# First products of two expert steps, moved into the attention stage's list

## The chip, the cores and the metric

The kernel is one program on one core of a Trainium2 chip. A core has five engines that run their own instruction lists in order and wait for each other by semaphores: TensorE (PE, matrix products; its weight loads are shown apart as PEld), VectorE (DVE), ScalarE (ACT), GpSimd (POOL) and SyncE (SP, which here only issues transfers, or DMAs). The metric is the device time of one execution in microseconds; lower is better. The kernel before ran at 891.88 us, the median of three runs (890.82, 891.88 and 893.85).

## What is computed

Three parts follow each other, all in fp32 accuracy:

```
attn_out = softmax(causal(q k^T / 8 + decay)) v        # 4 batches, 8 heads, 576 rows, 64 columns
x   = tokens: 2304 rows of 512
e   = argmax(x @ w_gate)                               # one of 8 experts for each token
x2  = weight(x, e) * (relu(x @ w1[e]) @ w2[e])         # 512 -> 1024 -> 512
out = (sigmoid(x2 @ w_gate2) * (x2 @ w_val)) @ w_out   # 512 -> 1536 -> 512
```

The tokens of an expert have to be gathered before its products: each token's row is written to a place that depends on how many tokens of that expert came before it, and rows are read back expert by expert.

## The kernel before, in words

**Attention stage** (`attention`, L740). The work of 16 pairs of heads is added to a list (`Flow.add`) with an assumed cost for each engine; a planner (`Flow.order`) then fixes one order for all engines, and `emit` writes it out. Pairs 12 to 15 are the last batch. When the last pair's `turn_x` (L436, writes `px`) and `scale` (L446, writes `xb`) are done, DVE adds up the expert logits and finds each token's expert (`first`, L591 to L596, the last of it a memset of `ohb`). PE then counts tokens per expert (`prefix`, L602 to L607, bf16 products into `px`), DVE turns the counts into places (`place`, L612 to L616) and weights (`weight`, L631 and L632), and POOL writes the rows of the last batch to `x_d` with five indirect DMAs (`scatter`, L647).

**Ahead of the experts.** After three batches the expert with most tokens so far is known. Its first 216 tokens (`AHEAD`) are fetched, turned and split into a high and a low half (`xah`, `xal`) while the attention stage still runs (`ahead_rows`), and so are the weights of its first three steps (`ahead_steps`: `wa0`, `wa1`, `wa2`).

**Expert stage** (`moe`, L963). It is written out in program order, not planned. A block is a group of tokens of one expert, a step is one eighth of the expert's 1024 hidden columns, and there are 72 steps. Block 0 (steps 0 to 7) is those 216 tokens, block 1 (steps 8 to 15) another 128 tokens of the same expert, among them tokens of the last batch. Step s is: `hidden(s)` (L1036, 12 products into `ph`: high by high, high by low, low by high, over four slices of 128), `relu(s)` (ACT L1042 writes `ha..h`, DVE L1043 `ha..l`), `split(s+2)` (ACT L986 and DVE L987 split a raw weight tile), `down(s-1)` (L1068 to L1070, 12 products into `py`). So PE runs hidden(0), hidden(1), down(0), hidden(2), down(1) and so on. Between these, DVE runs the some 35 small operations of `offsets` (L803 to L877), one at each `next(offsets)`.

**The queue of transfers.** `load(s)` (L981) reads the 512 KB of step s into one of three `raw` buffers, so it waits until `split(s-3)` has emptied its buffer. `fetch(1)` (L998) reads block 1's rows (`xr`) from `x_d` and waits for all scatters. Both are issued by SP, in order: a waiting transfer holds all that stand behind it. `weigh(1, 0)` (ACT L1008, writes `xg`) runs at step 6, `turn(1, 0)` (PE L1020) at step 7, ahead of down(6), and its result, split by ACT L1024 and DVE L1025 into `xh` and `xl`, is what hidden(8) multiplies.

Of the kernel before, what the change touches and what calls it, by code (L numbers as in the profile page):

```python
# [7 lines left out]
F32 = mybir.dt.float32  # L8
# [3 lines left out]
AF = mybir.ActivationFunctionType  # L12
ALU = mybir.AluOpType
# [3 lines left out]
P = 128  # L17
B, H, S, D = 4, 8, 576, 64
NP = B * H // 2
# [6 lines left out]
NK = DM // P  # L26
# [19 lines left out]
AHEAD = ((B - 1) * S + E - 1) // E  # L46
# [190 lines left out]
class Kern:  # L237
# [150 lines left out]
    def attn_pair(self, pr):  # L388


        nc, F, R = self.nc, self.F, self.R
        b, p = divmod(pr, NPB)
        i = pr % 2
        q, k = self.qk[pr]
# [34 lines left out]
        def finish(ts, oT, n):  # L429

            px = R["px"].new()

            def turn_x(e):
                for i in range(len(ts)):
                    for h in range(0, n, 64):
                        nc.tensor.matmul(px.t[h:h + 64, i], lhsT=oT.t[:, i * P + h:i * P + h + 64], rhs=self.w2[:, p],  # L436
                                         start=True, stop=True)
            F.add(turn_x, {"PE": 272 * len(ts)}, r=[oT, "w2"], w=[px], group=pr, kind="x", mode="columns")
            o = xb[:n, ts[0]:ts[-1] + 1, 2 * p:2 * p + 2, :]
            x = px.t[:n, 0:len(ts)].rearrange("p t (j c) -> p t j c", j=2)  # L440
            w = [("xb", b % 2, p, t) for t in ts]
            if ts[0] < 4:
                u = [2 * TORD.index(t) + j for t in ts for j in range(2)]

                def scale(e):
                    nc.vector.tensor_tensor(  # L446
                        out=o, in0=x, op=ALU.mult, in1=rs.t[:, u[0]:u[-1] + 1].rearrange(
                            "p (t j) -> p t j", j=2).unsqueeze(3).to_broadcast([P, len(ts), 2, XW]))
                F.add(scale, {"DVE": 70 + 166 * len(ts)}, r=[px] + [(rs, i) for i in u], w=w, group=pr, kind="scale")
            else:  # L450
                F.add(lambda e: self.copy(e, o, x), {"ACT": 190, "DVE": 240}, r=[px], w=w, group=pr, kind="x")
# [263 lines left out]
    def ahead_steps(self):  # L715
# [7 lines left out]
        for fb in range(NAHEAD):  # L723
# [8 lines left out]
            for i, cs in enumerate((slice(0, DM), slice(DM, 2 * DM))):  # L732
# [4 lines left out]
                    out=l, in0=raw[:, cs], in1=h.bitcast(F32), op=ALU.subtract),  # L737
                    {"DVE": 600, "POOL": 1230}, r=["raw", ("wah", fb, i)], w=[("wal", fb, i)], group=g)

    def attention(self, pool):  # L740
        ac, tmp = pool("ac", 1), pool("tmp", 1)
        F = self.F = Flow(PERIOD, SLACK)
        self.vt, self.qk, self.decay = {}, {}, {}
        spec = {
            "q": ([P, S], 3), "k": ([P, S], 3), "cb": ([P, 2, S], 2), "cm": ([P, 2, 512], 2), "ct": ([P, S], 2), "sc": ([P, 512], NSC), "sct": ([P, S], 1),
            "pt": ([P, 4, 2 * P], NPT), "ptt": ([P, 4, P], 1), "vt": ([P, 4, DM], 2),
            "oT": ([P, 2 * P], 2), "sums": ([P, 9], 3), "nmx": ([P, 9], 3), "rs": ([P, 9], 3),
            "lg": ([P, 5, 2 * E], 2), "m": ([P, 5], 2), "m2": ([P, 5], 2), "ls": ([P, 5, E], 2),
            "pos": ([P, 5, E], 2), "se": ([P, 5], 2), "so": ([P, 5, E], 2), "sel": ([P, 5], 2),
        }  # L750
        self.R = {n: Ring(pool(n, k), n, s, F32, k) for n, (s, k) in spec.items()}
        self.R["ohb"] = Ring(pool("ohb", 2), "ohb", [P, 5, E], BF16, 2)
        for n, s, k in (("px", [P, 2, 2 * XW], NPX), ("ps", [P, 512], NPS), ("tp", [P, 4, P], NTP), ("po", [P, 2 * P], NPO)):
            self.R[n] = Ring(pool(n, k, space=PSUM), n, s, F32, k)
        self.attn_setup(ac, tmp)
        for e in range(E):
            F.add(lambda e_, e=e: self.blank(e), {"SP": 700}, r=["zr"], w=["blank"], group=1 + e // 4, move=2500, after=35e3 + 5e3 * e)
        for i in range(4):
            F.add(lambda e, i=i: self.clear(i), {"SP": 700}, r=["zr"], w=["clear"], group=9 + i, move=2500, after=110e3 + 12e3 * i)
        for pr in range(NP + 2):  # L760
            if pr > 1:
                self.attn_pair(pr - 2)
            if pr < NP:
                self.attn_operands(pr)
        self.ahead_steps()
        F.emit()

    def unordered(self, key, ins):
# [194 lines left out]
    def moe(self, pools, preps):  # L963
        nc = self.nc
# [6 lines left out]
        raw, hs, ex, xg, py = {}, {}, {0: self.aex, 1: self.aex}, {}, {}  # L971
        w, xs = dict(enumerate(self.wa)), {0: self.xa}
        wbuf = self.wa + [[wp.tile([P, 2 * DM], F32R, name=f"w{n}{i}") for n in "hl"] for i in range(4 - NAHEAD)]

        def load(s):
            if s < len(steps):
                q, fb = steps[s]
                if q not in ex:
                    ex[q] = self.reg(self.orderi, blocks[q][2], ET.SP, E - 1)
                raw[s] = rawp.tile([P, 2 * DM], F32, name="raw")  # L980
                nc.sync.dma_start(out=raw[s], in_=self.words(ex[q], fb))  # L981
# [7 lines left out]
        def chunks(q):  # L989
            n = blocks[q][1]  # L990
            return [(c * P, min(n, (c + 1) * P)) for c in range((n + P - 1) // P)]

        def fetch(q):
            a0, _, r = blocks[q]
            row = self.reg(self.firsti, r, ET.SP, (E - 1) * NTOK) if r else self.arow
            for c, (a, b) in enumerate(chunks(q)):
                t = xg[q, c] = xp.tile([P, H, XW], F32, name="xr", bufs=NCH)
                ins = nc.sync.dma_start(  # L998
                    out=t[:b - a].rearrange("p h c -> p (h c)"), in_=self.x_d[bass.ds(row + (a0 + a), b - a)])
                self.after("scatter", ins)  # L1000

        def weigh(q, c):
            a, b = chunks(q)[c]
            t = xg[q, c]
            o = xg[q, c] = xp.tile([P, DM], F32, name="xg", bufs=3)
            o3, x3, g = o[:b - a].rearrange("p (h d) -> p h d", h=H), t[:b - a, :, 0:D], t[:b - a, 0, D:D + 1]
            if q == 1:
                nc.scalar.activation(o3, x3, AF.Copy, scale=g)  # L1008
            else:
                nc.gpsimd.tensor_scalar_mul(o3, x3, g)  # L1010
# [16 lines left out]
        def hidden(s):  # L1027
            q = steps[s][0]
            (wh, wl), (xh, xl), n = w[s], xs[q], blocks[q][1]
            ph = psH.tile([P, 512], F32, name="ph")  # L1030
            mm = []
            for k in range(NK):
                a, b = wh[:, k * P:(k + 1) * P], wl[:, k * P:(k + 1) * P]
                mm += [(a, xh[:, k, :n]), (a, xl[:, k, :n]), (b, xh[:, k, :n])]
            for i, (a, b) in enumerate(mm):
                nc.tensor.matmul(ph[:, :n], lhsT=a, rhs=b, start=i == 0, stop=i == len(mm) - 1)  # L1036
            return ph[:, :n]

        def relu(s, ph):
            n = blocks[steps[s][0]][1]  # L1040
            hh, hl = (t[:, :n] for t in self.ha[s % 2])
            nc.scalar.activation(hh, ph, AF.Relu)  # L1042
            nc.vector.scalar_tensor_tensor(  # L1043
                out=hl, in0=ph, scalar=0.0, in1=hh.bitcast(F32), op0=ALU.max, op1=ALU.subtract)
            hs[s] = hh, hl
# [46 lines left out]
        for s, (q, fb) in enumerate(steps):  # L1092
            if s >= NAHEAD - 1:
                load(s + 1 + NRAW)
            if s == 4:
                fetch(1)
            if (q, fb) == (nb - 1, 0):
                self.most = self.reg(self.nch, E, None, MAXCH)
            nq, c = q + 1, fb - (LATE, 3, 4)[min(q, 2)]
            if s == LATE or fb == 0 and 2 < nq < nb:  # L1100
                fetch(max(nq, 2))
            n = len(chunks(nq)) if nq < nb else 0
            ph = hidden(s)
            next(offsets, None)
            t = None
            if 0 <= c < n:
                t = turn(nq, c)
            early = 1 + (q > 1)
            if q and 0 <= c + early < n:
                weigh(nq, c + early)  # L1110
            relu(s, ph)
            if not q and 0 <= c + 1 < n:
                weigh(nq, c + 1)
            next(offsets, None)
            if t:
                land(*t)
            if s >= NAHEAD - 1:
                split(s + 2)
            if (q, fb) == (2, 2):
                prep = preps(lambda s: self.now >= due(s))  # L1120
            self.now = q, fb
            self.drip()
            if q > 1 and fb > 1:
                next(prep, None)
                if fb % 2:
                    next(prep, None)
            if flat:
                upright(*flat)
            flat = down(s - 1) if s else None
            next(offsets, None)  # L1130
# [525 lines left out]
```

## Time and profile before

| what | us |
|---|---|
| median of three runs | 891.88 |
| lowest, highest | 890.82, 893.85 |
| the profiled execution | 894.48 |
| its span, first to last instruction | 892.7 |
| PE busy in it | 851.7 (95%) |
| PE idle at the end of attention (217.4 to 219.85) | 2.50 |
| stretch behind it at half the granted clock | 6.55 |

All times of rows are microseconds from the start of the profiled span. A row of a timeline is one instruction, or several equal ones merged: start, duration, engine, source line, operation, what it writes and reads, and in square brackets how long the engine stood idle before it and what ended that. The granted clock is a share of TensorE's full 2.4 GHz, so 0.50 is 1.2 GHz.

### The profile page before, as it was taken

How to read it: one execution, taken by the hardware profiler on the slowest of the kernel's cores; microseconds unless marked ns; L12 is line 12 of the kernel's file. 1: busy time of each engine (PE TensorE's matmuls, PEld its weight loads, DVE VectorE, ACT ScalarE, POOL GpSimd, SP SyncE). 2: the span in 40 equal slices, each digit the busy share in tenths (PEclk: the TensorE clock that was granted, in tenths of full speed). 3: DMA queues.
4: the chain of work that ended last, by engine and by line, in shares of the span. 5: the costliest groups of instructions: out<-in, count | busy, mean ns of one | idle time of the engine just before them, and what ended most of it. 6: DMA issues, size and time to landing. Idle time of an engine off the chain costs nothing.

```text
span 892.7 us, 16050 instructions
## 1 busy us (share of the span) xinstructions
PE 851.7 (95%) x5664; PEld 751.5 (84%) x5664; DVE 617.7 (69%) x1439; ACT 449.0 (50%) x986; POOL 304.4 (34%) x380
## 2 busy tenths in 40 slices
PE   4999999998999999999989999999999999999996
PEld 3666667665999999999989888888999999999995
DVE  4767786877675767858747678889898996334454
ACT  3877777785464454646545544434343442332220
POOL 3211331221222222142125527375534466322113
PEclk9999999999999999999989999999999999999999
DMA  7799869543688677597644787757574557655531
GB/s 232 233 285 278 264 163 278 161 151 119 223 262 291 228 240 251 166 318 243 221 130 118 175 177 157 197 107 186 160 248 138 147 180 288 243 204 213 211 130 72
DMA packets 84987, 180.53 MB, mean 202 GB/s; under 512 B 10129, under 2 KB 47505, under 8 KB 83361
## 3 DMA queue, kind: packets, MB, share of 16 engines
q1 hardware_dynamic: 81345, 168.78, 62.4%
q0 software_dynamic: 3552, 10.63, 3.1%
q8 instruction: 47, 0.77, 0.4%
q14 instruction: 43, 0.35, 0.1%
HBM read 124.48 MB, written 54.90 MB: 201 GB/s over the span
## 4 chain that ended last, share of the span: by engine, by line
PE 34%; DVE 8%; issue 3%; ACT 2%; POOL 2%; DMA 1%; POOLq 0%; DVEq 0%; ACTq 0%; SPq 0%
PE po L1424 12%; PE x L1334 6%; PE w L1334 6%; PE z L1334 6%; PE y L1334 3%; DVE tt L1169 1%; DVE tt L1166 1%; DVE tt L1162 1%; DVE wt L1180 1%; POOL tt L1200 1%; ACT tt L1160 1%; POOL out L1432 1%; DMA raw<-in_wm 1%; DVE xs L1430 0%; DVE g0l L1387 0%
## 5 line engine op out<-in xcount | busy, mean ns | idle before, releaser
L1334 PE MATMUL x<-xo,wt 128*128 128x384 f32 x432 | 89.2, 341 | 7.4 <-DVEq L899 3.1
L1352 POOL TENSOR_TENSOR s<-s,s 128x384 f32<-128x384 f32 x36 | 40.7, 1129 | 153.5 <-ACT s L1351 153.5
L1334 PE MATMUL z<-xo,wt 128*128 128x384 f32 x432 | 87.8, 338 | 1.8 <-DVE r L1394 1.0
L1334 PE MATMUL w<-xo,wt 128*128 128x384 f32 x432 | 87.8, 338 | 1.3 <-DVE q L1374 1.0
L412 ACT ACTIVATE sc<-sc,nmx 128x512 f32<-128x512 f32 (+3 forms) x128 | 71.7, 563 | 33.6 <-DVE nmx L407 33.3
L1334 PEld LDWEIGHTS x<-xo,wt 128*128 128x128 f32 x432 | 77.2, 190 | 12.6 <-ACT s L1345 4.2
L1334 PEld LDWEIGHTS z<-xo,wt 128*128 128x128 f32 x432 | 76.8, 190 | 2.9 <-DVE r L1394 1.8
L1334 PEld LDWEIGHTS w<-xo,wt 128*128 128x128 f32 x432 | 76.7, 190 | 1.9 <-DVE q L1374 1.3
L1010 POOL TENSOR_SCALAR xg<-xr 128x512 f32<-128x512 f32 (+5 forms) x20 | 34.1, 1719 | 117.7 <-DMA xr<-x_d 117.7
L1424 PE MATMUL po<-wo,g1h 128*128 128x512 f32 x204 | 64.3, 397 | 0.0
L1200 POOL TENSOR_TENSOR tt<-tt 128x256 f32<-128x256 f32 x48 | 40.8, 858 | 57.3 <-DVE tt L1169 55.5
L1345 ACT COPY s<-x 128x384 f32<-128x384 f32 x36 | 17.3, 479 | 84.6 <-PE x L1334 77.2
L459 PE MATMUL tp<-ident,sc 128*128 128x128 f32 x320 | 53.6, 290 | 3.4 <-ACT pt L342 1.6
L342 ACT COPY pt<-tp 128x512 f32<-128x512 f32 (+3 forms) x128 | 49.5, 424 | 12.9 <-PE tp L459 12.3
L459 PEld LDWEIGHTS tp<-ident,sc 128*128 128x128 f32 x320 | 36.0, 143 | 21.1 <-ACT pt L342 8.1
L472 PE MATMUL ps<-k,q 64*128 64x512 f32 (+3 forms) x256 | 46.6, 476 | 6.0 <-DMA k<-in_kT 5.6
L1430 DVE TENSOR_TENSOR acc<-po,acc 128x512 f32<-128x512 f32 x60 | 39.7, 685 | 16.2 <-PE po L1424 16.1
L407 DVE CUSTOM_DVE_ANT_0 sc<-ps,cm 128x128 f32<-128x128 f32 x128 | 33.4, 286 | 19.2 <-PE tp L459 8.4
L1424 PEld LDWEIGHTS po<-wo,g1h 128*128 128x128 f32 x204 | 38.2, 188 | 7.7
L1355 DVE TENSOR_TENSOR s<-y,s 128x384 f32<-128x384 f32 x36 | 19.8, 551 | 35.1 <-PE y L1334 35.1
L407 DVE CUSTOM_DVE_ANT_0 sc<-ps,cb,nmx 128x384 f32<-128x384 f32 (+2 forms) x96 | 43.7, 479 | 0.3
L1334 PE MATMUL y<-xo,wt 128*128 128x384 f32 x216 | 43.4, 335 | 0.0
(325 smaller groups left out, 2444.8 us busy)
## 6 DMA issues: line engine op xcount, KB each, us to landing
raw<-in_w SPq DMA_DIRECT2D x69, 512.0 KB, 4.5
w_d<-wt SPq DMA_DIRECT2D x84, 256.0 KB, 5.4
wt<-w_d SPq DMA_DIRECT2D x12, 1792.0 KB, 7.4
raw<-in_wm SPq DMA_DIRECT2D x18, 1024.0 KB, 6.0
cb<-cum_d SPq DMA_DIRECT2D x32, 288.0 KB, 5.6
x_d<-roomf SPq DMA_DIRECT2D x8, 960.0 KB, 8.1
w_d<-wo SPq DMA_DIRECT2D x24, 256.0 KB, 6.1
wo<-w_d SPq DMA_DIRECT2D x6, 1024.0 KB, 8.3
```

What stands on the lines that cost most here:

```text
L342: self.nc.scalar.copy(out, in_)
L407: nc.vector.tensor_tensor_reduce(out=sc.t[:, cs], in0=ps.t[:, o:o + w], in1=in1(), scale=-0.125, scalar=acc if c else 3e38, op0=ALU.add, o ...
L412: F.add(lambda e: nc.scalar.activation(sc.t[:, :n], sc.t[:, :n], AF.Exp, bias=nmx.t[:, u:u + 1], scale=-1.0, accum_out=sums.t[:, u:u + 1]) ...
L459: nc.tensor.transpose(tp.t[:n, c - c0], sc.t[:, c * P:c * P + n], self.ident)
L472: nc.tensor.matmul(ps[j].t[:, :ext], lhsT=q.t[h, q0 + 64 * j:q0 + 64 * j + P], rhs=k.t[h, :ext], start=True, stop=True)
L1010: nc.gpsimd.tensor_scalar_mul(o3, x3, g)
L1200: nc.gpsimd.tensor_tensor(out=ts[:, o], in0=ts[:, a], in1=ts[:, b], op=ALU.subtract)
L1334: nc.tensor.matmul(bank, lhsT=l, rhs=r, start=first and not k and not i, stop=end and k == HK - 1 and i == 2, skip_group_check=True)
L1352: nc.gpsimd.tensor_tensor(out=s5, in0=s5, in1=s7, op=ALU.add)
L1355: nc.vector.tensor_tensor(out=s1, in0=y, in1=s1, op=ALU.add)
L1424: nc.tensor.matmul(po, lhsT=a, rhs=b, start=i == 0, stop=i == len(mm) - 1)
L1430: nc.vector.tensor_tensor(out=acc[i], in0=po, in1=acc[i], op=ALU.add)
```

## The change

The 24 products of hidden(0) and hidden(1), with their relus, become entries of the attention stage's list (`ahead_hidden`). They write `ps` buffers of the attention stage instead of `ph`, and they name the last pair's three `turn_x` results as inputs, so that they stand behind these. The expert stage takes the `ha` tiles as given for steps 0 and 1. `fetch(1)` is issued at step 3 instead of step 4.

```diff
-            F.add(turn_x, {"PE": 272 * len(ts)}, r=[oT, "w2"], w=[px], group=pr, kind="x", mode="columns")
+            F.add(turn_x, {"PE": 272 * len(ts)}, r=[oT, "w2"], w=[px, ("px", pr, ts[0])], group=pr,
+                  kind="x", mode="columns")
...
+    def ahead_hidden(self):
+        nc, F = self.nc, self.F
+        g = NP - 2
+        xh, xl = self.xa
+        for s in range(2):
+            (wh, wl), (hh, hl) = self.wa[s], (t[:, :AHEAD] for t in self.ha[s])
+            ps = self.R["ps"].new()
+            def mm(e, ps=ps, wh=wh, wl=wl):
+                ms = []
+                for k in range(NK):
+                    a, b = wh[:, k * P:(k + 1) * P], wl[:, k * P:(k + 1) * P]
+                    ms += [(a, xh[:, k]), (a, xl[:, k]), (b, xh[:, k])]
+                for i, (a, b) in enumerate(ms):
+                    nc.tensor.matmul(ps.t[:, :AHEAD], lhsT=a, rhs=b, start=i == 0, stop=i == len(ms) - 1)
+            F.add(mm, {"PE": 1350}, r=[("wah", s, 0), ("wal", s, 0)] + [(x, c) for x in ("xah", "xal") for c in range(2)] + [("px", NP - 1, t) for t in (0, 2, 4)],
+                  w=[ps], group=g)
+            F.add(lambda e, ps=ps, hh=hh: nc.scalar.activation(hh, ps.t[:, :AHEAD], AF.Relu),
+                  {"ACT": 360}, r=[ps], w=[("ha", s)], group=g)
+            F.add(lambda e, ps=ps, hh=hh, hl=hl: nc.vector.scalar_tensor_tensor(
+                out=hl, in0=ps.t[:, :AHEAD], scalar=0.0, in1=hh.bitcast(F32), op0=ALU.max, op1=ALU.subtract),
+                {"DVE": 390}, r=[ps, ("ha", s)], w=[("hl", s)], group=g)
...
         self.ahead_steps()
+        self.ahead_hidden()
         F.emit()
...
-            if s == 4:
+            if s == 3:
                 fetch(1)
...
-            ph = hidden(s)
+            ph = hidden(s) if s > 1 else None
...
-            relu(s, ph)
+            if ph is None:
+                hs[s] = tuple(t[:, :AHEAD] for t in self.ha[s])
+            else:
+                relu(s, ph)
```

All lines of the changed kernel below `turn_x` carry higher numbers (the new method and the new branches add 29 lines).

DVE's list at the routing of the last batch, before: from the memset of `ohb` (the last of finding the experts), over the sum `se`, the places (`pos`, `sli`, `base`) and the weight (the reciprocal), to the split of step 3's weights.

```order
L596 MEMSET ohb 64x4
L619 TENSOR_TENSOR ls<-lg,m 128x40
L622 CAST oh<-ohb 128x40
L623 TENSOR_TENSOR so<-ohb,lg 128x40
L624 TENSOR_REDUCE sel<-so 128x5
L627 TENSOR_REDUCE se<-ls 128x5
L628 TENSOR_SCALAR se<-se 128x5
L612 TENSOR_TENSOR pos<-px,base_175 128x40
...
L616 TENSOR_TENSOR base_176<-px,base_175 128x8
L631 SCALAR_TENSOR_TENSOR se<-sel,se 128x5
L632 RECIPROCAL xb_159<-se 128x5
```

The same place of the changed kernel's DVE list:

```order
L597 MEMSET ohb 64x4
L761 SCALAR_TENSOR_TENSOR ha0l<-ps,ha0h 128x216
L620 TENSOR_TENSOR ls<-lg,m 128x40
...
L625 TENSOR_REDUCE sel<-so 128x5
L613 TENSOR_TENSOR pos<-px,base_175 128x40
...
L617 TENSOR_TENSOR base_176<-px,base_175 128x8
L761 SCALAR_TENSOR_TENSOR ha1l<-ps,ha1h 128x216
L628 TENSOR_REDUCE se<-ls 128x5
L629 TENSOR_SCALAR se<-se 128x5
L632 SCALAR_TENSOR_TENSOR se<-sel,se 128x5
L633 RECIPROCAL xb_159<-se 128x5
```

The two low halves of the moved relus now stand inside the routing chain: one ahead of `ls`, one between the places and the sum `se`, which itself moved behind the places.

PE's list at the end of attention in the changed kernel (before, the counts L602 to L607 stood right behind `px`, and all 24 products behind the counts):

```order
L436 MATMUL px<-w_167,oT 64x160 x4
L756 MATMUL ps<-xah,wa0h 128x216
L756 MATMUL ps<-xal,wa0h 128x216
L756 MATMUL ps<-xah,wa0l 128x216
...
L756 MATMUL ps<-xah,wa1l 128x216
L603 LDWEIGHTS trib
L603 MATMUL px<-ohb,trib 128x40
...
L1094 MATMUL py_3628<-ha0h,wa0h 128x216
L1095 MATMUL py_3628<-ha0h,wa0l 128x216
L1096 MATMUL py_3628<-ha0l,wa0h 128x216
```

The products stand between the last `px` and the counts, and down(0) is the first thing behind the counts.

SP's list around block 1's fetch, before (the `raw` tiles are those of steps 6, 7, 8, then 9 and 10):

```order
L981 DMA raw_3645<-in_w12 128x1024
L981 ISA
L981 DMA raw_3680<-in_w12 128x1024
L981 ISA
L981 DMA raw_3717<-in_w12 128x1024
L998 ISA
L998 DMA xr_3719<-x_d 128x640
L981 ISA
L981 DMA raw_3755<-in_w12 128x1024
L981 ISA
L981 DMA raw_3789<-in_w12 128x1024
```

And in the changed kernel:

```order
L1007 DMA raw_3645<-in_w12 128x1024
L1007 ISA
L1007 DMA raw_3680<-in_w12 128x1024
L1024 ISA
L1024 DMA xr_3682<-x_d 128x640
L1007 ISA
L1007 DMA raw_3719<-in_w12 128x1024
L1007 ISA
L1007 DMA raw_3755<-in_w12 128x1024
```

The fetch, which waits for the scatters, now stands ahead of step 8's weights (raw_3719) instead of behind them.

## Rows read from the trace of the kernel before

**Rows 1.** The page: busy us, share of the span and instructions by engine.
```profile
PE 851.7 (95%) x5664; PEld 751.5 (84%) x5664; DVE 617.7 (69%) x1439; ACT 449.0 (50%) x986; POOL 304.4 (34%) x380
```

**Rows 2.** Stretches: length, busy us by engine, granted clock, DMA share, GB/s.
```profile
217.40:219.85 2.45, 0.00 (x0) 0.00 (x0) 2.05 (x10) 0.00 (x0) 0.00 (x0) 0.96 0.88 306
219.85:226.40 6.55, 6.55 (x39) 6.55 (x40) 4.19 (x20) 2.08 (x5) 3.95 (x6) 0.50 0.39 118
226.40:230.00 3.60, 3.60 (x34) 3.60 (x33) 1.13 (x5) 1.20 (x2) 2.02 (x4) 0.99 0.98 386
...
455.86:462.00 6.14, 6.14 (x19) 6.14 (x20) 1.64 (x2) 2.53 (x5) 0.00 (x0) 0.50 0.10 22
```

**Rows 3.** Timeline of PE, end of attention to block 1, and two later gaps.
```profile
219.85 0.21 PE L602 MATMUL px<-ohb,trib 128*128 128x40 bf16 x1 [2.50 <-DVE ohb L596]
220.01 0.27 PE L607 MATMUL px<-ohb,oneb 128*128 128x8 bf16 x5
...
237.99 0.28 PE L1036 MATMUL ph<-xah,wa2h 128*128 128x216 f32 x1
...
240.67 0.27 PE L1036 MATMUL ph<-xah,wh 128*128 128x216 f32 x1
...
244.00 0.33 PE L1036 MATMUL ph<-xl,wa0h 128*128 128x128 f32 x1
...
455.86 1.62 PE L1334 MATMUL x<-xo,wt 128*128 128x384 f32 x4 [3.11 <-DVEq L899]
...
541.44 1.34 PE L1334 MATMUL x<-xo,wt 128*128 128x384 f32 x6 [1.41 <-ACT s L1345]
```

**Rows 4.** Timeline of DVE, routing of the last batch and first splits.
```profile
219.74 0.06 DVE L596 MEMSET ohb<- 64x4 uint32 x1
...
220.38 0.18 DVE L627 TENSOR_REDUCE se<-ls 128x5 f32<-128x40 f32 x1
...
220.67 0.19 DVE L612 TENSOR_TENSOR pos<-px,base 128x40 f32<-128x40 f32 x1
...
221.67 1.23 DVE L987 TENSOR_TENSOR wl<-raw,wh 128x1024 fp32r<-128x1024 f32 x1
222.81 0.16 DVE L803 TENSOR_TENSOR cnt<-base,base 128x8 f32<-128x8 f32 x1
223.44 0.38 DVE L1043 SCALAR_TENSOR_TENSOR ha0l<-ph,ha0h 128x216 fp32r<-128x216 f32 x1 [0.47 <-ACT ha0h L1042]
223.74 0.15 DVE L806 SCALAR_TENSOR_TENSOR key<-cnt,erev 128x8 f32<-128x8 f32 x1
```

**Rows 5.** Timeline of ACT: routing, then `xg` and step 8's split.
```profile
220.06 0.24 ACT L637 ACTIVATE ls<-ls 128x40 f32<-128x40 f32 x1 [3.53 <-DVE ls L619]
...
239.77 0.71 ACT L1008 ACTIVATE xg<-xr 128x512 f32<-128x512 f32 x1
240.39 1.03 ACT L986 CAST wa0h<-raw 128x1024 fp32r<-128x1024 f32 x1
```

**Rows 6.** Timeline of POOL: first and last scatter of the last batch.
```profile
221.98 1.77 POOL L647 DMA_INDIRECT x_d<-xb,sli  x1 [13.71 <-DVE xb L632]
...
227.85 0.90 POOL L647 DMA_INDIRECT x_d<-xb,sli  x1 [0.23 <-issue]
```

**Rows 7.** SP's issues: weights of steps 7 and 8, then the fetch.
```profile
231.38 0.33 SPq L981 DMA_DIRECT2D raw<-in_w  x1
234.06 0.33 SPq L981 DMA_DIRECT2D raw<-in_w  x1
234.78 0.33 SPq L998 DMA_DIRECT2D xr<-x_d  x1
```

**Rows 8.** Issue to landing, us: all scatters; raw, 228 to 262; the fetch.
```profile
DMA to landing us min/median/max: 2.9/7.0/8.2
...
DMA to landing us min/median/max: 4.2/4.3/4.6
...
DMA to landing us min/median/max: 3.8/3.8/3.8
```

## The prediction

> **What bounds the kernel now.** I read the page first, then stretches around the seam between attention and experts, then the timelines there. PE is busy 851.7 of 892.7 us [rows 1], so what can still be won on PE is idle time and half-rate time. One place has both. From 217.35 to 219.85 PE does nothing for 2.50 us, until DVE's last memset of `ohb`, which ends at 219.80 [rows 3, 4]. Then the granted clock is 0.50, the 1.2 GHz level, for 6.55 us [rows 2], in which PE has work all the time. At half rate that work takes 6.55 us in place of 3.3, so the seam costs 2.5 + 3.3 = 5.8 us. The clock fell likewise behind the idle 3.11 us at 455.86, 6.14 us at 0.50, where four products of 384 columns take 1.62 us; behind 1.41 us at 541.44 six such take 1.34, so there it had not fallen [rows 2, 3].
>
> A second chain ends near the same place. From `ohb` it runs over counts, places, weight, five scatters, the fetch of block 1's rows, `xg`, turn(1, 0), `xh`, `xl` to hidden(8). In the trace PE meets it without a visible wait, since PE is late itself: hidden(8)'s second product, the first that needs `xl`, starts at 244.00 [rows 3]. If PE comes there earlier, this chain and the weights of step 8 decide.
>
> **The change, term by term.** I follow PE first, with nothing in its way.
>
> - The 24 products go into the idle time. 24 of them take one step's time at full rate, 237.99 to 240.67, 2.68 us [rows 3], so 12 take 1.34. They run from 217.35 to 220.03. Their inputs stand earlier in the lists than the last `px` (if one were late, that is the third rival below). The counts then wait for PE instead of DVE and start at 220.03 instead of 219.85, 0.18 late; they end after 0.43 (219.85 to 220.28 [rows 3]) at 220.46.
> - The clock stays at 1.00, as PE no longer stops. down(0) runs to 221.8. hidden(2) takes a `ph` bank that ha1l has to leave first; that is at 221.8 too (below).
> - Five steps of 2.68 later, at 235.2, hidden(7) starts. Before it was 240.67 [rows 3]. PE is 5.4 us ahead: 2.5 of idle and 3.3 of clock, less 0.4 for the counts and the seams.
>
> Next the routing chain, which the change lengthens. ha0l now stands ahead of `ls`: 0.30 (start to start, 223.44 to 223.74 [rows 4]). `pos` waits for the counts and starts at about 220.75 instead of 220.67, since the `se` pair (0.29, 220.38 to 220.67 [rows 4]) has left its place ahead of it. Behind the places come ha1l (0.30) and that pair (0.29). So the weight is 0.08 + 0.59 = 0.67 us late, and the first scatter goes at 222.65, not 221.98 [rows 6]. The two relus on ACT lie in its idle 3.53 us [rows 5] and cost nothing; without that cover it would be 0.35 each.
>
> The last scatter then issues at 227.85 + 0.67 = 228.5 [rows 6]. Its landing is not in the trace by itself; the shortest of all scatters is 2.9, the longest 8.2 [rows 8]. At 2.9 all rows are in `x_d` at 231.4. But the weights of step 7 now travel at the same time. Their buffer is freed by the split of step 4 on DVE: weight at 222.4, wl 1.14 (221.67 to 222.81), seven small operations of about 0.2 each (1.6 in all, an estimate from 0.16 and 0.15 and the gaps between such rows), a relu half 0.3, one more small one 0.2, the split 1.23 [rows 4]: 226.9. Before it was 231.38, when the scatters were through [rows 7]. While the scatters landed, the DMA engines were 98% busy at 386 GB/s [rows 2], so 512 KB more take 1.3 us. I put the scatters' end at 231.4 + 1.3 = 232.7; the ends are 231.4 and, with 8.2 for the last, 236.7. I stay near the short end, as the backlog ahead of the last piece is one transfer.
>
> The Trainium skill, DMA: Bandwidth & Descriptors, section Queues, rings and completion order, says that each DMA engine goes round-robin between the queues it has work for. By that rule SP's load and POOL's scatters share, and the 1.3 us are paid; if instead the scatters had the engines to themselves, their end would be 231.4. The 98% agree with the rule, but no row shows these two together in this order.
>
> fetch(1) was issued at 234.78 behind step 8's weights at 234.06 [rows 7]. Now it is first and goes at 232.8, but those weights stand behind a waiting fetch. Their buffer would be free about one step after that of step 7's, at some 229; they go 0.7 after it (234.06 to 234.78), at 233.5. So the edit to step 3 wins 2.0 us for the rows and next to nothing, 0.6, for the weights. Landings: rows 3.8 later, 236.6; weights 4.3 later, 237.8 [rows 8]. `xg` takes 0.62 (239.77 to 240.39 [rows 5]) and is done at 237.2; hidden(7) ends at 236.6, so turn(1, 0) waits 0.6. ACT splits step 8's weights at 237.8, not 240.39. From that cast to hidden(8)'s second product it was 244.00 - 240.39 = 3.6 us, through the DVE split, a relu half, `xh` and `xl`, all in the same order now. So that product starts at 241.4 instead of 244.00.
>
> **Sum.** 5.4 won ahead, 2.8 given back in new waits at turn(1, 0) and hidden(8): 2.6 us stay. The later blocks keep what they get; load(12) and the others behind step 8 move by the same 2.6. Against the profiled execution, 894.48, that is 891.9.
>
> The profiled execution is 2.6 above the median of 891.88, and the timed runs lie 3.0 apart, about the price of one half-rate stretch. So I can't take it that the median execution pays the 3.3 at 219.85. One that doesn't has hidden(8) at 244.0 - 3.3 = 240.7, and the change would make that 241.4, 0.7 worse. On the median the change is worth between -2.6 and +0.7; I take the middle, -1.0, as neither end has a row. **Forecast: 890.9 us**, its own range 889.2 to 892.6.
>
> **Rivals.**
>
> *The scatters aren't held up.* The weights of step 7 come too late or too thin to matter: scatters in at 231.4, all behind it 1.3 earlier, hidden(8)'s second product at 240.1, gain 2.6 + 1.3 = 3.9, 888.0. For it: the DMA share in the first part of the scatters is only 0.39 [rows 2], so there is room early. Against: 0.98 in the second part, where the load falls.
>
> *The clock falls at the new wait.* The waits at turn(1, 0) and hidden(8) come to 2.8 us with 12 products and one more between them. If TensorE drops to 0.50 there, it costs 3.1 to 3.3 as at the two places in the trace (half of 6.14 and 6.55 [rows 2]): 890.9 + 3.2 = 894.1, slower by 2.2, and slower by 3.9 (895.8) where the median had not paid before. It decides by the length: 2.50 and 3.11 us let it fall, 1.41 did not [rows 3]; here the idle is in pieces of 0.6, 0.9 and 1.5, but close together. The Trainium skill, TensorE: Matmul & The Clock Gate, section HAM oscillation — how this bites in real kernels, tells of kernels whose products come in bursts with waits for data between, and which pay the slow start again at every wait. By that rule this rival would be the outcome; the trace agrees for two of its gaps and not for the 1.41.
>
> *The idle time stays.* A wait that the trace doesn't show holds the 24 products (the planner's `ps` buffer, the three `px` inputs) until `ohb` is there: PE idles the 2.5 us as before and the clock falls, 891.9. Against: no input of theirs is late by the rows; or the loads of steps 9 to 12 eat the rest, with the same time.
>
> **How the numbers follow.** Forecast 0.50, scatters free 0.24, clock falls 0.20, idle stays 0.06. 0.3% of 891.88 is 2.7 us, about what a measurement of this kernel can tell from no change. Faster by more: 0.11 from the forecast, whose good end is at 889.2, and 0.20 from the second: 0.31. Slower by more: 0.10 from the third, 0.02 from the rest: 0.12. Within: 0.57. The range goes from the second case to the third, 887.8 to 894.1.
>
> **What would show it.** Right: no idle ahead of the counts and a clock of 1.00 from 217 to 235; hidden(7) at 235.2 or so; the first scatter 0.7 later; the fetch issued at 231.5 to 233, with step 8's weights right behind; a wait on PE ahead of hidden(8) of 1.5 to 3 us, released by DVE's `xl`, and hidden(8) at 240 to 241.5. Wrong: PE goes through hidden(8) without a wait (then the chain has slack that I don't see, and the gain is 5), or the granted clock is 0.50 behind it.

## The result and the profile after

The changed kernel runs at 898.09 us, the median of 14 runs (890.75 to 901.54), beside 892.49 for the kernel before in the same session (14 runs, 890.82 to 894.64). The ratio is 1.0052, 95% interval [1.0036, 1.0069]: slower by 0.5%, where 890.9 and a range up to 894.1 were forecast. The ratios here leave out an execution that is over 1.5% above the fastest of its kernel, and lie nearer to the quotients of the means (1.0053) than of the medians (1.0063). The profiled execution took 899.82 us, its span 898.0.

PE is busy 4 us longer than before [rows 1] with the same 5,664 instructions, so it worked more slowly, it did not work more:

```profile
PE 855.8 (95%) x5664; PEld 755.8 (84%) x5664; DVE 616.6 (69%) x1439; ACT 448.7 (50%) x986; POOL 305.5 (34%) x380
```

The stretches say where. The first three are those of [rows 2], the others lie behind hidden(8):

```profile
217.40:219.85 2.45, 2.45 (x31) 2.43 (x31) 2.15 (x13) 0.83 (x4) 0.00 (x0) 1.00 0.81 314
219.85:226.40 6.55, 6.55 (x60) 6.53 (x60) 6.07 (x24) 3.72 (x6) 4.14 (x5) 1.00 0.38 93
226.40:230.00 3.60, 3.60 (x35) 3.60 (x34) 2.74 (x7) 1.28 (x3) 2.95 (x6) 1.00 1.01 387
241.00:242.00 1.00, 0.64 (x5) 0.64 (x5) 0.90 (x2) 0.37 (x1) 0.00 (x0) 0.89 0.87 152
242.00:258.00 16.00, 16.00 (x69) 15.23 (x69) 7.13 (x15) 5.16 (x11) 4.68 (x3) 0.50 0.71 234
258.00:259.00 1.00, 1.00 (x7) 0.90 (x5) 0.74 (x2) 0.86 (x1) 0.00 (x0) 0.58 0.14 57
```

The idle time and the half rate of before are gone: PE is busy all of 217.40 to 219.85 and the granted clock (the last number but two) is 1.00 on to 241. Then it falls to 0.50, the 1.2 GHz level, and stays there for about 17 us, 69 matmuls in 16 us, with PE busy all the time. PE's timeline shows what stands ahead of that:

```profile
215.65 0.77 PE L436 MATMUL px<-w,oT 128*64 128x160 f32 x8 [0.52 <-ACT oT L342]
216.34 0.37 PE L756 MATMUL ps<-xah,wa0h 128*128 128x216 f32 x1
...
219.12 0.19 PE L603 MATMUL px<-ohb,trib 128*128 128x40 bf16 x1
...
234.29 0.28 PE L1062 MATMUL ph<-xah,wh 128*128 128x216 f32 x1
...
237.00 0.66 PE L1046 MATMUL tpm<-ident,xg 128*128 128x128 f32 x4 [1.20 <-ACT xg L1034]
...
239.61 0.33 PE L1062 MATMUL ph<-xh,wa0h 128*128 128x128 f32 x1 [0.63 <-ACT xh L1050]
...
241.36 0.33 PE L1062 MATMUL ph<-xl,wa0h 128*128 128x128 f32 x1 [1.42 <-DVE xl L1051]
...
267.48 0.31 PE L1062 MATMUL ph<-xh,wa0h 128*128 128x336 f32 x1
...
461.27 2.26 PE L1363 MATMUL x<-xo,wt 128*128 128x384 f32 x6 [3.32 <-DVEq L925]
```

Three waits, 1.20 at turn(1, 0), 0.63 and 1.42 at hidden(8), come to 3.25 us within 5.6 us. The last `px` row (L436) stands at 215.65, before at 216.59: attention ended 0.94 earlier. The change moves nothing ahead of it, and the row lies between 213.53 and 216.59 in the profiles of the two kernels and the first four experiments (e3_fetch3_only, whose edit comes later too, has 215.16). So I measure from that row on. To hidden(8)'s second product it is 25.71 us (before 244.00 - 216.59 = 27.41), 1.70 won. To hidden(16), the first row with 336 columns, it is 51.83; before it was 46.12, by these rows of the kernel before:

```profile
216.59 0.76 PE L436 MATMUL px<-w,oT 128*64 128x160 f32 x8 [0.52 <-ACT oT L342]
...
262.71 0.32 PE L1036 MATMUL ph<-xh,wa0h 128*128 128x336 f32 x1
```

Between the two products PE took 26.12 instead of 18.71: 7.41 lost at half rate. From there to 461.27 it lost 0.64, behind that it won 0.11. The sum, -0.94 - 1.70 + 7.41 + 0.64 - 0.11 = +5.3, is the difference of the spans, 898.0 - 892.7.

The chain that ends at hidden(8) begins with the routing. POOL's scatters, then the DVE and SP rows beside them:

```profile
221.82 1.70 POOL L648 DMA_INDIRECT x_d<-xb,sli  x1 [14.93 <-DVE xb L633]
223.83 0.96 POOL L648 DMA_INDIRECT x_d<-xb,sli  x1 [0.21 <-issue]
225.09 1.59 POOL L648 DMA_INDIRECT x_d<-xb,sli  x1 [0.22 <-issue]
226.98 1.51 POOL L648 DMA_INDIRECT x_d<-xb,sli  x1 [0.22 <-issue]
228.80 0.90 POOL L648 DMA_INDIRECT x_d<-xb,sli  x1 [0.21 <-issue]
```

```profile
221.46 1.20 DVE L1013 TENSOR_TENSOR wl<-raw,wh 128x1024 fp32r<-128x1024 f32 x1
...
224.50 1.20 DVE L1013 TENSOR_TENSOR wa0l<-raw,wa0h 128x1024 fp32r<-128x1024 f32 x1
...
226.43 1.23 DVE L1013 TENSOR_TENSOR wa1l<-raw,wa1h 128x1024 fp32r<-128x1024 f32 x1
```

```profile
233.31 0.33 SPq L1024 DMA_DIRECT2D xr<-x_d  x1
```

From the `px` row to the first scatter it is 6.17 us (before 221.98 - 216.59 = 5.39), to the fetch 17.66. Step 8's weights stand behind that fetch in SP's list and go at 233.89; they are cast from 237.79 on, and DVE forms `xl` only behind their split. So both inputs of hidden(8) hang on the fetch.

### The profile page after: what moved, and what is told of

It reads as the page before. It is cut to its first block, busy times and chain, and to the rows that moved or that the text cites. A ratio compares the mean times of both kernels' runs of the same rounds, so it can differ in the third digit from the quotient of the medians.

```text
span 898.0 us, 16051 instructions
## 1 busy us (share of the span) xinstructions
PE 855.8 (95%) x5664; PEld 755.8 (84%) x5664; DVE 616.6 (69%) x1439; ACT 448.7 (50%) x986; POOL 305.5 (34%) x380
## 5 line engine op out<-in xcount | busy, mean ns | idle before, releaser
L1459 DVE TENSOR_TENSOR acc<-po,acc 128x512 f32<-128x512 f32 x60 | 39.7, 685 | 16.2 <-PE po L1453 16.1
```

The source lines that it names most:

```text
L1459: nc.vector.tensor_tensor(out=acc[i], in0=po, in1=acc[i], op=ALU.add)
```

## The experiments

The first four kernels ran on a chip where the kernel before read 892.29, the others on two chips where it read 907.33 and 906.99; each is compared with the kernel before on its own chip. Below, "to hidden(8)" and "to hidden(16)" are counted from the last `px` row (L436) of the same profile, as above. A spare product is a matmul of 216 columns on `xah` into a `ph` buffer that nothing reads.

**Spare products in the new waits (e1_fill).** In the expert stage of the changed kernel:

```diff
+            if (q, fb) == (1, 0):
+                spare(18)
             ph = hidden(s) if s > 1 else None
...
+            if (q, fb) == (0, LATE):
+                spare(10)
             if 0 <= c < n:
```

> The changed kernel with spare products on TensorE in its two waits around step 8 (10 ahead of turn(1, 0), 18 ahead of hidden(8); 216 columns each, into a ph buffer that nobody reads). Theory A, the clock: what the change loses is the half-rate stretch of 17.0 us behind these waits (241.9 to 258.9). Then the granted clock stays at 1.00 from 220 to 262, hidden(8)'s second product still starts at about 241.4, and the time is some 8 us below the changed kernel's 898.1: 889 to 891. Theory B, the supply: rows and weights of block 1 come late, and PE would lose the time at full rate too. Then the stretch is gone, but the time stays within 2 us of 898.

Measured: 891.74 us (889.53 to 895.11), ratio 1.0000 [0.9985, 1.0016], 0.7 above the end of theory A's range. The last `px` row is at 215.20. PE's rows at hidden(8) and hidden(16), and the stretch between them:

```profile
241.55 0.33 PE L1062 MATMUL ph<-xl,wa0h 128*128 128x128 f32 x1 [0.33 <-DVE xl L1051]
...
259.66 0.31 PE L1062 MATMUL ph<-xh,wa0h 128*128 128x336 f32 x1
```

```profile
240.00:275.00 35.00, 34.42 (x248) 33.04 (x247) 24.08 (x40) 19.81 (x32) 11.75 (x6) 1.00 0.86 288
```

28 more matmuls made the kernel 6.4 us faster than the change. To hidden(8) it is even longer than in the changed kernel, 26.35, but the clock stays at 1.00 and hidden(16) follows at 44.46 instead of 51.83. This is the experiment that shows the cause. It also shows what the move is worth with the clock held: to hidden(16) it is 1.66 us less than before (46.12), and in the total, level with the kernel before, no gain can be told.

**The fetch back at step 4 (e2_fetch4).** The change without its edit to `fetch(1)`:

```diff
-            if s == 3:
+            if s == 4:
                 fetch(1)
```

> The changed kernel with the fetch of block 1 back at step 4, behind step 8's weights. My account: these weights go at about 227.7 instead of 233.9, the fetch still at 233 to 234 since the scatters hold it, so hidden(8) waits for xg, xh and xl alone: about 239.7 instead of 241.4, with waits of 1.2 and under 1.0 on PE. If the length of the waits decides on the clock, it falls in fewer executions, 891 to 895. If the place of the fetch doesn't matter, 897 to 899 and the same rows.

Measured: 894.07 (891.86 to 901.83), ratio 1.0041 [1.0016, 1.0066], five of the 12 runs at 895.5 to 901.9. In the profiled one (892.96) there is one long wait, at turn(1, 0), and the fall that comes with it is short:

```profile
236.57 1.12 PE L1046 MATMUL tpm<-ident,xg 128*128 128x128 f32 x4 [2.89 <-ACT xg L1034]
```

```profile
236.00:240.00 4.00, 3.43 (x17) 0.57 0.59 164
240.00:260.00 20.00, 19.45 (x148) 1.00 0.82 266
```

(Here PE alone is listed: length, busy us, granted clock, DMA share, GB/s.) The fetch:

```profile
232.54 0.33 SPq L1024 DMA_DIRECT2D xr<-x_d  x1
```

That is 19.01 us after `px` (213.53), 1.35 later than in the change: step 8's weights, issued at 225.57, now travelled beside the scatters. So hidden(8) comes at 26.50, later than in the change (25.71), where I had expected it 1.7 sooner. The times are as expected, and the moved products bring a loss without the edit to the fetch; that edit changes the shape of the wait, not its being there.

**The fetch alone (e3_fetch3_only).** The kernel before with one number changed:

```diff
-            if s == 4:
+            if s == 3:
                 fetch(1)
```

> The kernel before with the fetch at step 3 alone. PE comes to hidden(8) at 244.0 as before; the fetch goes at 231 to 232, step 8's weights at 234 as before. So no change by my account: 892.5, within 1. If the order of the two transfers is what hurts, 894 to 898.

Measured: 892.39, ratio 0.9999 [0.9984, 1.0014]; idle 2.51 us ahead of the counts and half rate behind it, as before. PE doesn't wait for the fetch there, so nothing is won.

**Spare products ahead of the counts (e4_spare).** The kernel before with 24 spare products where the change puts its 24: the clock is held at the old place, and nothing is moved. Its method is the change's `ahead_hidden` with the same inputs named and without the relus, and with this as its product:

```diff
+                for i in range(12):
+                    nc.tensor.matmul(ps.t[:, :AHEAD], lhsT=xh[:, i % NK, :P], rhs=xh[:, i % NK], start=True, stop=True)
```

> The kernel before with 24 spare products (216 columns, their output is read by nobody) in the idle time ahead of the expert counts; hidden(0) and hidden(1) stay behind the counts. It takes the idle time away and nothing else. If the half-rate stretch behind it is what the idle time costs, the clock stays at 1.00 from 217 to 240, hidden(8) comes 3 us earlier, and the time is 889 to 890. If the median execution doesn't pay for that stretch, or the rows of block 1 bound hidden(8), 891.5 to 893.

Measured: 892.35 (890.09 to 901.91), ratio 1.0011 [0.9984, 1.0038]. Nine of the 12 runs lie at 890.1 to 893.1, with a mean granted clock of 0.991 to 0.996, three at 900.6 to 901.9, with 0.983 to 0.985. The profiled one is of the three (901.67). PE's waits at turn(1, 0) and hidden(8), and the stretch behind them:

```profile
238.15 0.66 PE L1034 MATMUL tpm<-ident,xg 128*128 128x128 f32 x4 [0.52 <-ACT xg L1022]
...
241.56 0.33 PE L1050 MATMUL ph<-xl,wa0h 128*128 128x128 f32 x1 [1.35 <-DVE xl L1039]
```

```profile
243.00:264.00 21.00, 21.00 (x91) 19.84 (x91) 9.99 (x17) 7.83 (x14) 5.70 (x3) 0.51 0.59 192
```

The same fall, some 10 us dear (the means of the two groups are 901.4 and 891.6), without any moved product: what brings it is PE coming to hidden(8) early and waiting there.

**Spare products at all three places (e5_all).** The kernel before with both edits, the 24 of e4_spare and the 10 and 18 of e1_fill:

```diff
+            if (q, fb) == (1, 0):
+                spare(18)
             ph = hidden(s)
```

> The kernel before (products of steps 0 and 1 where they were) with 24 spare products ahead of the counts, 10 ahead of turn(1,0) and 18 ahead of hidden(8), all on rows that lie in SBUF anyway, so that TensorE has no idle stretch of over half a microsecond there. It asks what the moved products themselves are worth once the clock is held. Theory A (the clock is all there is to the result, and the chain scatter, fetch, xl sets hidden(8) whatever TensorE does ahead of it): no half-rate stretch between 212 and 275, last px to hidden(16) near the 44.5 us of the changed kernel with spare products, time 891.3 to 892.3. Theory B (the 24 products that the change moves ahead are worth their own time once the clock is held): hidden(8) 2 us or more later than there, time near 894.

Measured: ratio 0.9993 [0.9973, 1.0014], clock 1.00 from 225 to 290. Theory A in the time, not quite in the stage: to hidden(8) it is 27.66 us and to hidden(16) 45.66, 1.3 and 1.2 more than with the moved products (e1_fill; theory B had 2 or more). That is too little for the total to show.

**Two of the three waits (e8_late).** The change with the 18 spare products alone, none ahead of turn(1, 0):

```diff
+            if (q, fb) == (1, 0):
+                spare(18)
             ph = hidden(s) if s > 1 else None
```

> The changed kernel with spare products (18) ahead of hidden(8) alone; the wait of 1.2 us ahead of turn(1,0) stays. Theory A1 (the two waits at hidden(8), 0.63 and 1.42 us close together, bring the clock down): no half-rate stretch behind it in the profile, time 891.5 to 892.5. Theory A2 (all the idle time from turn(1,0) on counts, wherever it lies): the clock falls in some or most of the executions, and the median lies between 894 and 898.

Measured: ratio 1.0003 [0.9987, 1.0019], as theory A1 had it. Waits of 1.22 and 0.81 us, 4.9 us apart, left the clock at 1.00:

```profile
250.87 0.66 PE L1046 MATMUL tpm<-ident,xg 128*128 128x128 f32 x4 [1.22 <-ACT xg L1034]
...
255.74 0.33 PE L1062 MATMUL ph<-xl,wa0h 128*128 128x128 f32 x1 [0.81 <-DVE xl L1051]
```

```profile
225.00:290.00 65.00, 61.27 (x498) 57.88 (x495) 42.65 (x101) 31.67 (x58) 17.19 (x16) 1.00 0.76 246
```

**Spare products inside the fall (e10_dense).** The change with the 18 ahead of hidden(10) instead:

```diff
-            if (q, fb) == (1, 0):
+            if (q, fb) == (1, 2):
                 spare(18)
```

> The changed kernel with 18 spare products of 216 columns ahead of hidden(10), in the middle of the stretch at half rate, where TensorE otherwise runs products of 128 columns. It asks what sets the 17.0 us for which the clock stays low. L1 (what TensorE runs behind the wait sets it): the clock is back at full by about 252, half rate for 10 us or less, and the 18 products (3.3 us at half rate) cost nothing in all, time 895 to 898. L2 (the length doesn't depend on what runs): half rate until about 259 as in the changed kernel, hidden(16) later by some 2 to 3 us, time 900 to 901. If the clock does not fall in this execution, it tells neither.

Measured: waits as in the change (1.33, 0.46, 1.42), half rate for some 10 us:

```profile
255.00:266.00 11.00, 11.00 (x55) 10.71 (x53) 5.13 (x11) 3.00 (x6) 5.71 (x3) 0.53 0.80 265
```

One execution, 913.05, 5.7 us above the kernel before there. The stretch is as L1 had it, but e12_short and e7_small7 below have shorter ones than the change too, without these products, so it is a hint and no more.

**The low halves behind the routing (e6_behind).** The change with 10 and 14 spare products and one other edit:

```diff
-                {"DVE": 390}, r=[ps, ("ha", s)], w=[("hl", s)], group=g)
+                {"DVE": 390}, r=[ps, ("ha", s)], w=[("hl", s)], group=SPARE)
```

(`SPARE` is the planner's group for operations that it places only where they delay no other.) With that, DVE has ha0l and ha1l right behind the reciprocal and ahead of `wl`.

> The changed kernel with 10 spare products ahead of turn(1,0), 14 ahead of hidden(8) (18 before), and VectorE's two low halves of the moved steps put behind the routing's last operation instead of among its operations. Theory A (routing chain sets the scatters, they set the fetch, the fetch sets hidden(8), and the clock is held): last px to the first scatter 5.4 us as in the kernel before (6.2 in the changed one), hidden(8) 0.4 to 0.7 us sooner after the last px than the 26.35 us of the first kernel with spare products, time 891.0 to 891.4, below both kernels. Rival (the scatters end when the transfers beside them let them): first scatter sooner, the fetch's issue not, time as there, 891.7; if the 4 products fewer uncover a wait and the clock falls, about 898.

Measured: ratio 0.9990 [0.9973, 1.0008], not told from 1. The first scatter 5.41 us after `px`, the fetch 16.51 (17.66 in the change), but hidden(8) at 26.43, no sooner. The new wait and the spare products kept PE late:

```profile
233.37 0.37 PE L1096 MATMUL py<-ha0l,wa0h 128*128 128x216 f32 x1 [1.24 <-DVE ha0l L761]
```

Theory A fails for hidden(8): the chain was early, and now PE set the time. So the spare products could go.

**The same order without spare products (e11_order).** The changed kernel with that one edit alone.

> The changed kernel with one edit and no spare products: VectorE's two low halves of the moved steps stand behind the routing's reciprocal instead of among the routing's operations. The profile of the kernel with this order and spare products says what follows: scatters issued in 0.96 to 1.09 us each from 5.4 us after the last x product on, fetch 16.5 us after it (17.66 in the changed kernel), TensorE with a new wait of 1.2 us at down(0) for the first low half. Theory A (the chain routing, scatters, fetch sets the waits at step 8, and waits this short leave the clock alone): no wait ahead of turn(1,0), 0.5 to 0.9 us in all at hidden(8), its second product 24.3 to 24.8 us after the last x product (25.71 in the changed kernel, 27.41 before), no half-rate stretch behind it, time 1.5 to 3 us below the kernel before. Rival (whatever is gained ahead of hidden(8) comes back as idle time or at half rate): the wait at hidden(8) stays over 1.4 us, the clock falls there in most executions, time about 0.5% above the kernel before.

Measured: 904.70 beside 906.99, ratio 0.9973 [0.9953, 0.9992]. Scatters from 5.40 us on, fetch 16.54, to hidden(8) 24.52, to hidden(16) 43.17 (before 46.12):

```profile
229.07 0.76 PE L436 MATMUL px<-w,oT 128*64 128x160 f32 x8 [0.52 <-ACT oT L342]
...
234.50 0.37 PE L1096 MATMUL py<-ha0l,wa0h 128*128 128x216 f32 x1 [1.24 <-DVE ha0l L761]
...
250.89 0.60 PE L1046 MATMUL tpm<-ident,xg 128*128 128x128 f32 x4
...
253.59 0.33 PE L1062 MATMUL ph<-xl,wa0h 128*128 128x128 f32 x1 [0.70 <-DVE xl L1051]
...
272.24 0.32 PE L1062 MATMUL ph<-xh,wa0h 128*128 128x336 f32 x1
```

```profile
250.00:290.00 40.00, 38.89 (x283) 37.54 (x282) 26.17 (x42) 23.21 (x38) 10.71 (x6) 1.00 0.89 295
```

All as theory A had it. PE's idle time is spread, 1.24 early and 0.70 late, the clock holds, and this version beats both kernels: 0.27% below the one before, where the change on the same chip is 0.6% above (after_again).

**Why two scatters took longer (e12_short, e7_small7).** In the change, once the low halves of step 4's and 5's weights are cut to 64 columns, once step 7's weights to 256 (there `few` is 256 for s == 7, in the load and in both halves of the split):

```diff
+                few = 64 if s in (4, 5) else 2 * DM
-                nc.vector.tensor_tensor(out=tl, in0=raw.pop(s), in1=th.bitcast(F32), op=ALU.subtract)
+                nc.vector.tensor_tensor(out=tl[:, :few], in0=raw.pop(s)[:, :few], in1=th[:, :few].bitcast(F32), op=ALU.subtract)
```

> The changed kernel with the low halves of step 4's and step 5's weights formed for 64 of 1,024 columns only (the rest of them keeps older numbers). It asks why two scatters took 1.59 and 1.51 us to issue instead of 0.96. Theory P (a scatter that starts while VectorE runs one of these differences of two SBUF operands is held until that ends): the five issues take 1.70, 0.96, 0.96, 0.96 and 0.90 us, the last ends 12.8 us after the last x product (14.05 in the changed kernel), the fetch is issued 16.4 to 17.0 us after it (17.66). Theory W (the transfers of step 7's weights slow them, as the prediction had it): issues and fetch as in the changed kernel, 17.5 to 17.8 us.

> The changed kernel with step 7's weights cut to 256 of 1,024 columns, load and splitting both (the rest of them keeps older numbers). Theory W (step 7's transfer, issued 0.65 us after the third scatter, slows the scatters' landing): scatter issues as in the changed kernel, fetch 16.4 us after the last x product or little more, 1.3 us sooner than there (17.66). Theory P (VectorE's differences hold the issues, and the landings follow them): the issues 1.70, 0.96, 1.59, 1.51 and 0.90 us as before, fetch 17.2 to 17.7 us.

Measured in e12_short, scatters and fetch:

```profile
233.78 1.70 POOL L648 DMA_INDIRECT x_d<-xb,sli  x1 [14.95 <-DVE xb L633]
235.79 0.96 POOL L648 DMA_INDIRECT x_d<-xb,sli  x1 [0.22 <-issue]
237.06 0.96 POOL L648 DMA_INDIRECT x_d<-xb,sli  x1 [0.21 <-issue]
238.32 0.96 POOL L648 DMA_INDIRECT x_d<-xb,sli  x1 [0.23 <-issue]
239.58 0.90 POOL L648 DMA_INDIRECT x_d<-xb,sli  x1 [0.23 <-issue]
```

```profile
245.39 0.33 SPq L1025 DMA_DIRECT2D xr<-x_d  x1
```

The issues are as theory P said, 12.88 us to the end of the last, but the fetch comes 17.79 us after `px` (227.60), not sooner than in the changed kernel on the same chip (after_again, 243.60 - 226.02 = 17.58). In e7_small7 the issues took 1.70, 0.96, 1.59, 1.50 and 0.90, and the fetch, at 243.40 with `px` at 226.57, comes after 16.83, 0.75 sooner than there. So each theory has half: scatters issued beside VectorE's differences take longer (P), but shorter issues don't bring the fetch forward; fewer bytes beside the scatters do (W), and more, in e2_fetch4, put it back by 1.35. Step 7's weights cost the landing 0.75 us or a little more, as a quarter of them was still there. One thing blurs e12_short: the shorter differences free step 7's buffer sooner, so its load goes 9.10 us after `px` (236.70), in after_again 10.10. One execution each: 905.75 with half rate for some 3 us, 907.60 with about 14.

**The change once more (after_again).** The changed kernel on the chip of e11_order, e12_short and e7_small7.

> The changed kernel itself, beside the others on this chip. Theory A (the clock falls at hidden(8) in most executions): median 0.3 to 0.7% above the kernel before, a half-rate stretch of 10 to 20 us from hidden(8) on where the profile shows waits of 3 us there. Rival (what was measured belongs to one chip): within 0.3% of the kernel before.

Measured: 913.51 us, the median of 12 runs (902.90 to 917.92), ratio 1.0059 [1.0032, 1.0087], waits of 1.16, 0.73 and 1.42 and half rate for about 17 us again:

```profile
252.00:270.00 18.00, 18.00 (x82) 17.13 (x81) 8.40 (x16) 6.02 (x11) 5.19 (x3) 0.53 0.67 214
```

The result doesn't belong to one chip.

## Why the prediction was wrong, point by point

- **The bound and the lead.** Right. The idle time and the half rate at the old place went; hidden(7) began at 234.29, forecast 235.2, and with attention 0.94 earlier that is 5.4 us of lead, as worked out.
- **The routing chain.** 0.67 forecast, 6.17 - 5.39 = 0.78 measured. e6_behind and e11_order show that it is the two low halves: with them behind the reciprocal it is 5.41 and 5.40.
- **The scatters and the fetch.** The fetch was forecast at 232.8, 16.2 us after `px`; it came at 17.66. The last scatter went 13.15 us after `px` (228.80), forecast 11.9 (228.5): 0.1 of that is the routing, the rest two scatters that took some 0.6 longer to issue each, which I had not seen. From it to the fetch it was 4.5, forecast 4.3 (2.9 + 1.3, and 0.1 to the issue). That looks right but is partly luck: with short issues, in e12_short, it was 5.8 and the fetch no sooner. What the runs bear out is the direction of the term for transfers beside the scatters, in e7_small7 (0.75 us or more for step 7's weights) and e2_fetch4 (1.35 for step 8's); 512 KB at 386 GB/s are 1.36, I had 1.3.
- **Step 8's weights and hidden(8).** The cast that splits them began at 237.79, forecast 237.8, and from it to hidden(8)'s second product it was 3.57, forecast 3.6. Counted from `px` both are 0.9 later than forecast; the early end of attention hid that. Waits of 3.25 us, forecast 2.8 (its pieces, 0.6, 0.9 and 1.5, add up to 3.0). So the lead was given back much as forecast, 1.7 us kept instead of 2.6.
- **The step that failed** is the clock behind the new waits. The sum charged these waits with their length alone, 2.8 us, and put a fall of the clock behind them at nothing. What the runs showed there is 17 us at 0.50 and 7.41 us lost between hidden(8) and hidden(16), and e1_fill, with the waits filled, loses neither. The fall stood only in the rival "the clock falls at the new wait", whose mechanism is what happened and whose chance and price were too small. I gave it 0.20 because of a length: a stop of 1.41 us had left the clock alone [rows 3], and the new waits come in pieces. But 1.20, 0.63 and 1.42 us close together brought it down, in e4_spare 0.52 and 1.35 did, in e7_small7 0.40, 0.33 and 1.42, while 1.22 and 0.81 (e8_late) or 0.70 (e11_order) did not, in one profiled execution each. The Trainium skill, TensorE: Matmul & The Clock Gate, section HAM oscillation — how this bites in real kernels, tells of bursts of products with waits for data between, and of a slow start again behind each wait, in an example whose waits are longer than these; the trace here agrees for these three waits, with the 1.00 ahead of 241 and the 0.50 behind, and e8_late's two don't. I weighed the one row, of 1.41, above the rule.
- **The price.** I took 3.1 to 3.3 us from two stretches of 6 to 7 us at half rate [rows 2], as if the length of a fall were a property of the chip. Here it was 17 us, 7.4 us lost to hidden(16), and the median of the change lies 6.4 us above e1_fill, where it doesn't fall. With 7.4 in place of 3.2 the rival's sum reads 890.9 + 7.4 = 898.3, beside 898.09 measured. Even at my own price its paragraph had 895.8 for a median that had not paid before, and I ended the range at 894.1.
- **The median.** That some executions pay a fall and others don't was right, but I used it to make the gain smaller (-1.0), not to make the loss possible: the changed kernel's lowest run is 890.75 and its highest 901.54. Four of its 14 executions have a mean granted clock of 0.990 to 0.994 and take 890.75 to 895.14, the other ten have 0.980 to 0.988 and take 896.03 to 901.54; e4_spare's runs stand in two groups likewise.
- **"The scatters aren't held up"** fell with the fetch at 233.31 (its time reads 888.0 in its paragraph and 887.8 in the range; nothing hangs on that). **"The idle time stays"** fell with the products at 216.34.

What stays open is why the half-rate stretch lasts 17 us here, 20 in e4_spare, 3 in e2_fetch4 and e12_short, 10 in e10_dense and 14 in e7_small7, and why the same kernel has executions without one. TensorE was busy in all of them, but for the wait in e2_fetch4. Block 1's products have 128 columns instead of 216, and e10_dense put wider ones among them, but e7_small7 and e12_short are shorter without that, so no run here tells it.

## What to carry to other kernels

Work that is moved into an idle stretch brings the engine sooner to its next wait; before the move, ask how long that wait will be, and where TensorE is concerned add what a fall of the clock behind it may cost. Its length in the trace of before (6.55 us) is no bound for it at another place (17). Look whether the chain behind that wait can be shortened with the same edit: here the two small VectorE operations that came along stood in it, and putting them behind the routing turned a loss of 0.5 to 0.6% into a gain of 0.27%. And where a wait can't be shortened, it may be cheaper to spread it (e11_order has 1.24 us early and 0.70 late), or even to fill it with products that nobody needs (e1_fill), than to let TensorE stand.

## What was not expected of the hardware

A scatter's issue on POOL took 0.96 us (the last 0.90) where no VectorE difference of two SBUF tiles (L1013) was under way at its start, and longer where one was: 1.59 at 225.09 in the change. Such an issue ends 0.8 to 1.0 us behind the difference (225.09 + 1.59 = 226.68; the one at 224.50 ended at 225.70), so it seems to begin only then. e12_short made two of the differences short, and both long issues went. The Trainium skill, SBUF — State Buffer, section SBUF: two separate sides, says that VectorE and GpSimd share a pair of ports as an exclusive lock, held for a whole instruction by whichever starts first, where a VectorE operation with two SBUF inputs meets a GpSimd operation that reads SBUF; the scatters' rows agree. VectorE's side of it they don't show: the difference at 224.50 began inside the issue of 223.83 and took 1.20 us like the others. The first scatter of the kernel before, 1.77 us [rows 6], fits too: it began 0.31 behind the start of the difference at 221.67 [rows 4].
